# Gated linear attention and a squared-ReLU layer: the first chunks' loads interleave the batches over the partitions, and their q and k are turned by identity matmuls

## The chip, the cores and the metric

The kernel runs on one core of one Trainium2 chip. The core has a matmul engine (TensorE, PE, with a separate row PEld for its weight loads), a vector engine (DVE), a scalar engine (ACT), GpSimd (POOL) and SyncE (SP), on whose queue all the DMAs here are issued. The engines run side by side and wait for each other by semaphores. The metric is the device time of one execution in microseconds.

## The reference

Two stages. The first is a recurrence for 4 batches, 8 heads, 768 steps and head dimension 48: the state of a head (48x48) is scaled by rows with alpha, the outer product of k and v is added, and the output is q times the state. The second takes the 3072 tokens of 384 values through a layer of 2048 hidden values:

```python
for t in range(S):
    state = alpha[:, :, t, :, None] * state + np.einsum('bhd,bhe->bhde', k[:, :, t], v[:, :, t])
    y[:, :, t] = np.einsum('bhd,bhde->bhe', q[:, :, t], state)
x = y.transpose(0, 2, 1, 3).reshape(B * S, H * D)
out = np.maximum(x @ w_in, 0) ** 2 @ w_out
```

All inputs and the output are fp32 in device memory.

## The kernel before

The 768 steps of a batch are cut into 6 chunks of 128, which makes 24 chunks in all. Within a chunk the recurrence is solved by matmuls. With the running sum of ln(alpha), q is multiplied by its exponential A and k by the exponential of its negative (Ainv). The scores of all pairs of steps are then a matmul of the two products, a mask (`utri_b`) keeps the earlier steps, and the masked scores times v give the output (`py`). A state per batch carries the rest from chunk to chunk. The matmul needs the products with the head dimension on the partitions, so each product is turned by TensorE first, into PSUM, and copied to SBUF as bf16 (`qkT`).

The second stage (`add_moe1`, `add_moe2`) takes a chunk's output, turned into `xT_big`, through w_in (48 matmuls of 128 columns per chunk), relu on ACT, the square on DVE, and w_out (16 matmuls of 384 columns per chunk). Both weights are loaded as fp32 blocks (`load_w`, L297) into a pool `stage` of 5 buffers and cast to bf16 (`e_cast`, L316) by GpSimd, DVE or ACT.

The first chunk of each of the four batches (chunks 0 to 3) is treated jointly, and this is where the change lies. These four chunks need no state from before. `add_joint_load` (L357) loads alpha, q and k of all four into three tiles `atJ`, `qtJ`, `ktJ` of 128 partitions, four transfers each. A partition holds four consecutive steps of one batch (r = 0 to 3, next to each other, so each piece read is 4x48 fp32 = 768 bytes), and partition 32b+i holds batch b, steps 4i to 4i+3. Each transfer thus fills 32 neighbouring partitions:

```python
src = SRC4[nm][:, :, 0:P, :].rearrange("b h (i r) d -> b i h (r d)", r=JN)
pin(nc.sync.dma_start(out=J[nm][JP * b:JP * b + JP], in_=src[b]))
```

`add_joint` (L366) then works on all batches at once: two Ln on ACT (L371), four running sums (one for each r) by matmuls with the masks `le_b` and `lt_b`, which hold the order of steps inside each batch's block of partitions, eight exponentials on ACT (L409), eight products on DVE (L414). Each product (r and q or k) is turned by four transposes (one for each pair of heads), into one bf16 PSUM tile, and one copy (L428 on ACT, L430 on DVE) brings the tile to `qkT_j`. In `qkT_j` the columns of a batch run by step, 4i+r, so the copy for one r writes every fourth bf16 element.

`add_chunk` goes on for each chunk: the scores (`e_p2`), the masking of their two halves (`e_sm`, L588, on DVE; for chunks 1 and 3 the second half goes by an ACT copy and a GpSimd mask instead, as `SMP` says), the output, its cast `xn`, its turn and `xT_big` (L549, L551). `add_shuffle` (L439) moves k's joint products by DMA to one tile per batch, which the state of the batch needs.

The order is written out by a planner that runs while the program is built (`Plan`, L76). Every operation has an engine or a choice of engines, a duration, what it depends on, which PSUM bank it takes and a priority. The planner plays them through in time and fixes the order on each engine: on an engine, of the operations that can start first, the one with the lowest priority number. `DMA_ORDER` fixes the order of the loads on SP. In front of the first matmul, and in gaps of its plan before the second stage has begun, it puts matmuls on a zero tile (`warm`). PSUM has eight banks: two for scores (`ps_sc`), one for the state, five that are handed out (`banks`).

Of the kernel before, what the change touches and what calls it, by code (L numbers as in the profile page):

```python
# [156 lines left out]
def kernel(  # L157
# [38 lines left out]
    ps_sc = ctx.enter_context(tc.tile_pool(name="ps_sc", bufs=1, space=PSUM))  # L196
    ps_st = ctx.enter_context(tc.tile_pool(name="ps_st", bufs=1, space=PSUM))
    banks = [ctx.enter_context(tc.tile_pool(name=f"bank{i}", bufs=1, space=PSUM)) for i in range(5)]
# [18 lines left out]
    sel4 = consts.tile([P, 64], BF16)  # L217
    nc.gpsimd.tensor_copy(le_b, utri_f)
    nc.gpsimd.affine_select(
        out=lt_b, in_=le_b, compare_op=ALU.is_ge, fill=0.0,  # L220
        base=-1, pattern=[[1, P]], channel_multiplier=-1,
    )
    for b in range(JN - 1):
        blk = slice(JP * b, JP * b + JP)
        nc.vector.memset(le_b[blk, JP * b + JP:], 0.0)
        nc.vector.memset(lt_b[blk, JP * b + JP:], 0.0)
    nc.vector.memset(sel4, 0.0)  # L227
    for b in range(JN):
        nc.vector.memset(sel4[JP * b:JP * b + JP, b:b + 1], 1.0)
# [42 lines left out]
    sl_sc = Slots(1)  # L272
# [21 lines left out]
    W_CUT = {"i": [0, 2, 4, 8, 12, 16], "o": [0, 4, 8, 12, 16]}  # L294
    SB = 5

    def load_w(which):  # L297
        j = len(w_ready[which])
        lo, hi = W_CUT[which][j:j + 2]
        n = hi - lo  # L300
        box = {}

        def halves(t):
            return t.rearrange("p j (a f) -> p a j f", a=2) if which == "i" else t
        if which == "i":
            src, dst = w_in_r[:, :, lo * P:hi * P], w_in_b[:, :, lo * P:hi * P]
            shape = [P, KT, n * P]
        else:
            src, dst = w_out_r[:, lo:hi, :], w_out_b[:, lo:hi, :]
            shape = [P, n, d_model]  # L310

        def e_issue():
            box["w"] = stage.tile(shape, FP32, name=f"w{which}{n}", tag="stage")
            pin(nc.sync.dma_start(out=box["w"], in_=src))

        def e_cast():  # L316
            if op.eng == "POOL":
                pin(nc.gpsimd.tensor_copy(dst, box["w"]))
            elif op.eng == "DVE":
                pin(nc.vector.tensor_copy(halves(dst), halves(box["w"])))  # L320
            else:
                pin(nc.scalar.copy(dst, box["w"]))
        prev = w_cast[-SB] if len(w_cast) >= SB else None
        ld = add("DMA", WLD * n / 4 + 0.03, e_issue, prev, lat=2.0)
        op = add({"POOL": 0.1 + 0.46 * n, "DVE": 0.1 + 0.2 * n, "ACT": 0.1 + 0.32 * n}, 0, e_cast, ld, prio=-3.0)
        w_cast.append(op)
        w_ready[which].append(op)
# [9 lines left out]
    SC_BANKS = [sl_sc, Pair(sl_bank[2], sl_bank[3])]  # L337
    sl_sc.bank = None
    SMP = (1, 3)
    EARLY_BANKS = sl_bank[0:4]  # L340
# [16 lines left out]
    def add_joint_load(nm):  # L357
        src = SRC4[nm][:, :, 0:P, :].rearrange("b h (i r) d -> b i h (r d)", r=JN)

        def ld(b):  # L360
            if b == 0:
                J[nm] = stage.tile([P, H, JN * D], FP32, name=nm + "J", tag="stage")
            pin(nc.sync.dma_start(out=J[nm][JP * b:JP * b + JP], in_=src[b]))  # L363
        J["ld_" + nm] = [add("DMA", JLD, lambda b=b: ld(b), lat=2.0, at=0.6) for b in range(JN)]

    def add_joint():  # L366
# [7 lines left out]
        def e_tot():  # L374
            J["tot"] = psum(tot, [P, 512], FP32)
            for p in range(NP):
                for r in range(JN):
                    mm(J["tot"][:, JN * p:JN * (p + 1)], lhsT=L_j[:, r, 2 * p:2 * p + 2, :], rhs=sel4[:, 0:JN],
                       start=(r == 0), stop=(r == JN - 1), skip_group_check=True)
        tot = plan.add(Op("PE", 0.42, e_tot, lns, prio=-9.0, takes=GLA_BANKS, lat=0.05))  # L380
# [5 lines left out]
        x0 = add("ACT", 0.19, lambda: e_ae(0), tot, prio=-9.0)  # L386
        J["ae"] = tot.gives = add("ACT", 0.19, lambda: e_ae(1), tot, after(x0), prio=-9.0)

        ends = {"q": [], "k": []}

        def add_turn(r):
# [9 lines left out]
            for key, sc, prod, nm, j0 in (("q", 1.0, qA_j, "qt", 0), ("k", -1.0, kI_j, "kt", NP)):  # L401
                a, end = add_half(r, d, p0, a, key, sc, prod, nm, j0)
                ends[key].append(end)
            p0.gives = a

        def add_half(r, d, p0, a, key, sc, prod, nm, j0):
# [3 lines left out]
            a_ = add("ACT", 0.38, e_A, p0, *([after(a)] if a else []), prio=-10.0 + r * 0.001)  # L410
# [4 lines left out]
            m = add({"DVE": 0.47, "POOL": 0.95} if (key, r) in POOL_MUL else "DVE", 0.47, e_mul, a_, *J["ld_" + nm], prio=-10.0 + r * 0.001)  # L415
            J["use_" + nm] = m

            def e_tr():
                d["p" + key] = psum(tp, [P, 2 * NP, P], BF16)
                for p in range(NP):  # L420
                    tr(d["p" + key][:, p, :], prod[:, r, 2 * p:2 * p + 2, :], ident_bf)
            tp = plan.add(Op("PE", 0.22, e_tr, [m], takes=EARLY_BANKS, prio=-10.0 + r * 0.001, lat=0.15))

            def e_cp():
                o = qkT_j[:, j0:j0 + NP].rearrange("p j b (i r) -> p j b i r", r=JN)[:, :, :, :, r]
                i = d["p" + key][:, 0:NP, :].rearrange("p j (b i) -> p j b i", b=JN)
                if cp.eng == "ACT":
                    pin(nc.scalar.copy(o, i))  # L428
                else:
                    pin(nc.vector.tensor_copy(o, i))  # L430
            cp = add({"ACT": 0.49, "DVE": CPJ}, 0, e_cp, tp, prio=-10.0 + r * 0.001)
            tp.gives = cp
            return a_, cp
        for r in range(JN):
            add_turn(r)
        J["T"] = ends["q"] + ends["k"]
        w_cast.extend([lns[-1], J["use_qt"], J["use_kt"]])

    def add_shuffle(b):  # L439
        def sh():  # L440
            pin(nc.sync.dma_start(out=kn(b), in_=kI_j[JP * b:JP * b + JP]))
        J["kn", b] = [add("DMA", 0.38, sh, J["use_kt"], lat=2.0)]
# [90 lines left out]
    def add_chunk(s):  # L533
# [36 lines left out]
        def e_p2():  # L570
            x = getattr(p2.slot, "slots", None)
            if x is None:
                sc = ps_sc.tile([P, 2, NP, P], FP32, name="sc")
                sc = [sc[:, 0], sc[:, 1]]
            else:
                sc = [banks[sl.bank].tile([P, NP, P], FP32, name=f"bank{sl.bank}") for sl in x]
            d["sc"] = sc
# [5 lines left out]
        p2 = d["p2"] = plan.add(Op("PE", 0.42, e_p2, J["T"] if joint else [cp], takes=SC_BANKS if joint else [sl_sc], lat=0.10, **g))  # L583
# [76 lines left out]
    M2_LAST = sl_bank[::-1]  # L660
# [92 lines left out]
    DMA_ORDER = ["at", "qt", "kt", (0, "vt"), (1, "vt"), "i", (2, "vt"), "i", (3, "vt"), "i", "i", "i", "sh0", "sh1", "sh2", "sh3", "o", "o", 4, "o", "o", 5]  # L753
# [61 lines left out]
    for _ in range(7):  # L815
        mm(wp, lhsT=warm[:, 0:P], rhs=warm, start=True, stop=True)
    pe_end = WARM_END
# [43 lines left out]
```

## Time and profile before

| | |
|---|---|
| median of 3 runs | 196.13 us (195.58 to 196.45) |
| the profiled execution | 195.68 us, span 194.0 us |
| busy, share of the span | PE 95%, PEld 72%, DVE 67%, ACT 65%, POOL 11% |
| chain that ended last | PE 86%, DMA 6%, ACT 3%, DVE 1% |
| read from device memory, written | 25.17 MB, 4.72 MB |
| first matmul with w_in, first with w_out | 25.31 us, 37.21 us from the span's start |
| end of the last matmul | 190.1 us |

The page divides the span into 40 slices of 4.85 us and gives the busy tenths of each engine. The row PEclk is the clock that TensorE was granted, in tenths of full speed. A row of the groups names the line, the engine, the operation, the tile written and the tiles read with their shapes, the count, and after the bar the busy time in us, the mean ns of one, and the idle time before them with its cause. The chain of waits lists start, length, and what it was. Times in it are us from the start of the span. Matmul ends are modelled; an engine that is idle but not awaited costs nothing.

### The profile page before, as it was taken

Reading aid. Unit: us, or ns where it says so; the run is one execution under the profiler, and the core shown is the slowest. Engines: PE = TensorE matmul, PEld = TensorE weight load, DVE = VectorE, ACT = ScalarE, POOL = GpSimd, SP = SyncE. Lnnn points to the kernel's source line nnn. Section 1 sums busy time; section 2 is a strip of 40 time slices with the busy share of each in tenths; the row PEclk is TensorE's granted clock in tenths of the full one; section 3 lists DMA queues with packets and bytes.
Section 4 is the critical chain, followed back from the end, with each engine's and each line's share of the span. In section 5 each row is a group of like instructions: output and inputs, shape, how many; then the busy total and the mean of one; then the engine's idle time right before and its main releaser. Section 6 shows DMA issues by size and latency. Waiting matters only on the chain.

```text
span 194.0 us, 5260 instructions
## 1 busy us (share of the span) xinstructions
PE 184.6 (95%) x2103; PEld 140.4 (72%) x2103; DVE 130.6 (67%) x278; ACT 126.8 (65%) x285; POOL 21.4 (11%) x45
## 2 busy tenths in 40 slices
PE   7678899999999999999999999999999999999992
PEld 2446699866897787967867868868868768768660
DVE  2058698884899897967858758787767757735100
ACT  2389598924897588976956955954955846718210
POOL 8004520101101111111210110110110000000000
PEclk9997999999999999999999999999999999999999
DMA  6999999799999998999989899751110110111111
GB/s 127 208 201 277 351 377 272 169 329 176 208 249 208 179 217 168 230 177 219 204 175 222 175 211 235 143 129 39 41 45 0 46 42 3 41 41 44 40 57 66
DMA packets 98793, 30.75 MB, mean 159 GB/s; under 512 B 88144, under 2 KB 97616, under 8 KB 98768
## 3 DMA queue, kind: packets, MB, share of 16 engines
q1 hardware_dynamic: 98768, 30.42, 67.6%
q8 instruction: 16, 0.26, 0.6%
q14 instruction: 9, 0.07, 0.1%
HBM read 25.17 MB, written 4.72 MB: 154 GB/s over the span
## 4 chain that ended last, share of the span: by engine, by line
PE 86%; DMA 6%; ACT 3%; DVE 1%; SPq 1%; issue 0%; DVEq 0%
PE bank L266 74%; PE bank L269 7%; DMA ktJ<-in_k_dram 4%; PE sc L266 4%; ACT gT L428 3%; DMA atJ<-in_alpha_dram 2%; PE st L266 2%; DVE sm L588 1%; SPq L363 1%; DVE gT L414 0%; ACT xT_big L549 0%; ACT ob L744 0%; ACT ae_j L385 0%; DVEq L414 0%
## 5 line engine op out<-in xcount | busy, mean ns | idle before, releaser
L266 PE MATMUL bank<-xT_big,w_in_b 128*128 128x256 bf16 (+1 forms) x720 | 76.5, 251 | 0.0
L266 PE MATMUL bank<-w_out_b,gT 128*128 128x384 bf16 x384 | 71.8, 326 | 0.0
L692 ACT ACTIVATE r<-bank 128x512 bf16<-128x512 f32 x96 | 56.7, 604 | 16.4 <-PE bank L266 14.4
L266 PEld LDWEIGHTS <-w_in_b 128*128 128x128 bf16 x720 | 55.2, 98 | 4.9
L266 PEld LDWEIGHTS <-gT 128*128 128x128 bf16 (+1 forms) x432 | 36.4, 97 | 19.9 <-ACT gT L428 0.8
L702 DVE TENSOR_TENSOR gT<-r 128x512 bf16<-128x512 bf16 x96 | 39.8, 433 | 15.8 <-ACT r L692 15.5
L588 DVE TENSOR_TENSOR sm<-sc,utri_b 128x512 bf16<-128x512 f32 x44 | 28.2, 682 | 3.4 <-PE sc L266 3.3
L563 POOL CAST vb<-vt 128x384 bf16<-128x384 f32 x21 | 11.8, 563 | 117.3 <-DMA vt<-in_v_dram 66.2
L744 ACT COPY ob<-bank 128x384 f32<-128x384 f32 x21 | 10.1, 483 | 19.7 <-PE bank L266 19.6
L508 DVE TENSOR_TENSOR qA_s<-qt,A 128x384 bf16<-128x384 f32 x20 | 11.1, 557 | 9.6 <-ACT A L489 9.5
L551 DVE COPY qkT<-bank 128x1024 bf16<-128x1024 bf16 x20 | 13.8, 689 | 5.5 <-PE bank L269 5.4
L463 ACT CAST sb<-st 128x384 bf16<-128x384 f32 x20 | 9.5, 476 | 8.2 <-DVE st L458 8.2
L549 ACT CAST xn<-bank 128x384 bf16<-128x384 f32 x24 | 11.6, 481 | 4.5 <-PE bank L266 4.4
L266 PEld LDWEIGHTS <-qkT 64*128 64x128 bf16 (+1 forms) x240 | 10.0, 95 | 5.6 <-issue 2.4
L266 PE MATMUL bank<-warm 128*128 128x256 bf16 (+1 forms) x59 | 12.7, 361 | 1.3 <-DVE sel L227 1.3
L489 ACT ACTIVATE A<-bank 128x384 bf16<-128x384 f32 x20 | 10.0, 500 | 4.3 <-PE bank L266 4.2
L556 ACT ACTIVATE L_s<-at 128x384 bf16<-128x384 f32 x20 | 10.4, 522 | 1.9 <-DMA at<-in_alpha_dram 1.6
L511 DVE TENSOR_TENSOR kI_s<-kt,Ainv 128x384 bf16<-128x384 f32 x20 | 11.0, 551 | 0.0
L266 PEld LDWEIGHTS <-warm 128*128 128x128 bf16 x59 | 6.7, 121 | 4.7 <-issue 2.2
L493 ACT ACTIVATE Ainv<-bank 128x384 bf16<-128x384 f32 x20 | 10.1, 504 | 0.0
L266 PEld LDWEIGHTS <-sm 128*128 128x128 bf16 x192 | 8.5, 96 | 1.8 <-issue 0.3
L551 DVE COPY xT_big<-bank 128x384 bf16<-128x384 bf16 x21 | 7.3, 350 | 3.6 <-PE bank L269 3.6
(74 smaller groups left out, 173.7 us busy)
## 6 DMA issues: line engine op xcount, KB each, us to landing
vt<-in_v_dram SPq DMA_DIRECT2D x24, 192.0 KB, 4.0
out_dram<-ob SPq DMA_DIRECT2D x24, 192.0 KB, 3.0
at<-in_alpha_dram SPq DMA_DIRECT2D x20, 192.0 KB, 4.0
qt<-in_q_dram SPq DMA_DIRECT2D x20, 192.0 KB, 4.0
kt<-in_k_dram SPq DMA_DIRECT2D x20, 192.0 KB, 3.7
wo<-in_moe_w_out_dram SPq DMA_DIRECT2D x4, 768.0 KB, 7.8
wi<-in_moe_w_in_dram SPq DMA_DIRECT2D x3, 768.0 KB, 7.9
atJ<-in_alpha_dram SPq DMA_DIRECT2D x4, 192.0 KB, 3.9
```

The source lines that it names most:

```text
L266: pin(nc.tensor.matmul(*a, **kw))
L269: pin(nc.tensor.transpose(*a))
L493: pin(nc.scalar.activation(d["Ai"], d["pm"][:, 0:HD].rearrange("p (h d) -> p h d", h=H), AF.Exp, scale=-1.0))
L508: pin(nc.vector.tensor_mul(qA[:, :, 0:D], d["qt"], d["A"]))
L511: pin(nc.vector.tensor_mul(kI[:, :, 0:D], d["kt"], d["Ai"]))
L549: pin(nc.scalar.copy(out_t, in_t))
L551: pin(nc.vector.tensor_copy(out_t, in_t))
L556: pin(nc.scalar.activation(L[:, :, 0:D], d["at"], AF.Ln))
L563: pin(nc.gpsimd.tensor_copy(d["vb"], d["vt"]))
L588: pin(nc.vector.tensor_mul(d["sm"][:, hh], d["sc"][hh], utri_b.to_broadcast([P, NP, P])))
L692: pin(nc.scalar.activation(box["r"][:, 0:w], box["ph"][:, 0:w], AF.Relu))
L702: pin(nc.vector.tensor_mul(gT[g][:, f0:f0 + per, lo * P:lo * P + n], r, r))
```

## The change

The joint tiles interleave the batches: partition 4i+b holds batch b, steps 4i to 4i+3, so a transfer fills every fourth partition. The masks `le_b` and `lt_b` follow: a matmul of a small tile `own` with itself gives 1 where two partitions are of the same batch, and DVE multiplies this with the triangle. `sel4` is now the last four columns of `le_b`.

The turn works by pair of heads instead of by r: for q or k and one pair, four identity matmuls (one for each r) write into one fp32 PSUM tile, each to every fourth column, so that the columns stand in the order of steps; one copy then brings 128x512 fp32 to contiguous bf16. Each such group needs all four products of q or of k. The priorities put q's products ahead of k's, and the totals of the chunks (`tot`) behind all of them.

The scores lose their own pool: `banks` has seven entries, scores use banks 5 and 6 as a pair, and the running sums and turns at the start may use them too. All masks are made on DVE (`SMP` is empty). The third block of w_in is cut into two, and the planner may not put the first three casts of w_in on ACT, nor the first two on DVE (the list `w_cast` already holds three entries then), so the first two go to GpSimd.

```diff
@@ -193,9 +193,8 @@

-    ps_sc = ctx.enter_context(tc.tile_pool(name="ps_sc", bufs=1, space=PSUM))
     ps_st = ctx.enter_context(tc.tile_pool(name="ps_st", bufs=1, space=PSUM))
-    banks = [ctx.enter_context(tc.tile_pool(name=f"bank{i}", bufs=1, space=PSUM)) for i in range(5)]
+    banks = [ctx.enter_context(tc.tile_pool(name=f"bank{i}", bufs=1, space=PSUM)) for i in range(7)]

@@ -214,19 +213,13 @@
     lt_b = consts.tile([P, P], BF16)
-    sel4 = consts.tile([P, 64], BF16)
-    nc.gpsimd.tensor_copy(le_b, utri_f)
+    own = consts.tile([JN, JP, JN], BF16)
+    nc.gpsimd.memset(own, 0.0)
     nc.gpsimd.affine_select(
-        out=lt_b, in_=le_b, compare_op=ALU.is_ge, fill=0.0,
-        base=-1, pattern=[[1, P]], channel_multiplier=-1,
+        out=own, in_=own, compare_op=ALU.not_equal, fill=1.0,
+        base=0, pattern=[[0, JP], [1, JN]], channel_multiplier=-1,
     )
-    for b in range(JN - 1):
-        blk = slice(JP * b, JP * b + JP)
-        nc.vector.memset(le_b[blk, JP * b + JP:], 0.0)
-        nc.vector.memset(lt_b[blk, JP * b + JP:], 0.0)
-    nc.vector.memset(sel4, 0.0)
-    for b in range(JN):
-        nc.vector.memset(sel4[JP * b:JP * b + JP, b:b + 1], 1.0)
+    sel4 = le_b[:, P - JN:P]
     ones_t = consts.tile([P, 32], BF16)
@@ -269,7 +262,6 @@
     plan = Plan()
-    sl_sc = Slots(1)
     sl_bank = [Slots(1) for _ in banks]
@@ -291,8 +283,10 @@
     w_cast = []
-    W_CUT = {"i": [0, 2, 4, 8, 12, 16], "o": [0, 4, 8, 12, 16]}
+    W_CUT = {"i": [0, 2, 4, 6, 8, 12, 16], "o": [0, 4, 8, 12, 16]}
     SB = 5
+    NO_ACT = 6
+    NO_DVE = 5

@@ -322,7 +316,12 @@
         ld = add("DMA", WLD * n / 4 + 0.03, e_issue, prev, lat=2.0)
-        op = add({"POOL": 0.1 + 0.46 * n, "DVE": 0.1 + 0.2 * n, "ACT": 0.1 + 0.32 * n}, 0, e_cast, ld, prio=-3.0)
+        on = {"POOL": 0.1 + 0.46 * n, "DVE": 0.1 + 0.2 * n, "ACT": 0.1 + 0.32 * n}
+        if len(w_cast) < NO_DVE:
+            del on["DVE"]
+        if len(w_cast) < NO_ACT:
+            del on["ACT"]
+        op = add(on, 0, e_cast, ld, prio=-3.0)
         w_cast.append(op)
@@ -334,10 +333,10 @@
     POOL_MUL = ()
-    SC_BANKS = [sl_sc, Pair(sl_bank[2], sl_bank[3])]
-    sl_sc.bank = None
-    SMP = (1, 3)
-    EARLY_BANKS = sl_bank[0:4]
+    EARLY_BANKS = sl_bank[0:4] + sl_bank[5:7]
+    SC = Pair(sl_bank[5], sl_bank[6])
+    SC_BANKS = [SC, Pair(sl_bank[2], sl_bank[3])]
+    SMP = ()
     EARLY = 4
@@ -360,7 +359,7 @@
                 J[nm] = stage.tile([P, H, JN * D], FP32, name=nm + "J", tag="stage")
-            pin(nc.sync.dma_start(out=J[nm][JP * b:JP * b + JP], in_=src[b]))
+            pin(nc.sync.dma_start(out=J[nm][b::JN], in_=src[b]))
         J["ld_" + nm] = [add("DMA", JLD, lambda b=b: ld(b), lat=2.0, at=0.6) for b in range(JN)]
@@ -375,18 +374,15 @@
                 for r in range(JN):
-                    mm(J["tot"][:, JN * p:JN * (p + 1)], lhsT=L_j[:, r, 2 * p:2 * p + 2, :], rhs=sel4[:, 0:JN],
+                    mm(J["tot"][:, JN * p:JN * (p + 1)], lhsT=L_j[:, r, 2 * p:2 * p + 2, :], rhs=sel4,
                        start=(r == 0), stop=(r == JN - 1), skip_group_check=True)
-        tot = plan.add(Op("PE", 0.42, e_tot, lns, prio=-9.0, takes=GLA_BANKS, lat=0.05))
+        tot = Op("PE", 0.42, e_tot, lns, prio=-9.0, takes=GLA_BANKS, lat=0.05)

...
             pin(nc.scalar.activation(ae_j[rows, :, :, j], t, AF.Exp))
-        x0 = add("ACT", 0.19, lambda: e_ae(0), tot, prio=-9.0)
-        J["ae"] = tot.gives = add("ACT", 0.19, lambda: e_ae(1), tot, after(x0), prio=-9.0)
-
-        ends = {"q": [], "k": []}
+        muls = {"q": [], "k": []}

@@ -398,47 +394,58 @@
             a = None
-            for key, sc, prod, nm, j0 in (("q", 1.0, qA_j, "qt", 0), ("k", -1.0, kI_j, "kt", NP)):
-                a, end = add_half(r, d, p0, a, key, sc, prod, nm, j0)
-                ends[key].append(end)
+            for key, sc, prod, nm in (("q", 1.0, qA_j, "qt"), ("k", -1.0, kI_j, "kt")):
+                a = add_half(r, d, p0, a, key, sc, prod, nm)
             p0.gives = a

-        def add_half(r, d, p0, a, key, sc, prod, nm, j0):
+        def add_half(r, d, p0, a, key, sc, prod, nm):
+            g = dict(prio=-10.0 + r * 0.001 + (0.01 if key == "k" else 0.0))
+
             def e_A():
...
                 pin(nc.scalar.activation(d["A" + key], d["pm"][:, 0:HD].rearrange("p (h d) -> p h d", h=H), AF.Exp, scale=sc))
-            a_ = add("ACT", 0.38, e_A, p0, *([after(a)] if a else []), prio=-10.0 + r * 0.001)
+            a_ = add("ACT", 0.38, e_A, p0, *([after(a)] if a else []), **g)

...
                 pin(e.tensor_mul(prod[:, r, :, 0:D], J[nm][:, :, r * D:(r + 1) * D], d["A" + key]))
-            m = add({"DVE": 0.47, "POOL": 0.95} if (key, r) in POOL_MUL else "DVE", 0.47, e_mul, a_, *J["ld_" + nm], prio=-10.0 + r * 0.001)
+            m = add({"DVE": 0.47, "POOL": 0.95} if (key, r) in POOL_MUL else "DVE", 0.47, e_mul, a_, *J["ld_" + nm], **g)
             J["use_" + nm] = m
+            muls[key].append(m)
+            return a_
+
+        def add_turned(key, p, prod, j0):
+            g = dict(prio=(-9.97 if key == "q" else -9.96) + p * 0.001)
+            d = {}

             def e_tr():
-                d["p" + key] = psum(tp, [P, 2 * NP, P], BF16)
-                for p in range(NP):
-                    tr(d["p" + key][:, p, :], prod[:, r, 2 * p:2 * p + 2, :], ident_bf)
-            tp = plan.add(Op("PE", 0.22, e_tr, [m], takes=EARLY_BANKS, prio=-10.0 + r * 0.001, lat=0.15))
+                d["pT"] = psum(tp, [P, JN * P], FP32)
+                for r in range(JN):
+                    o = d["pT"].rearrange("p (b i r) -> p r i b", b=JN, r=JN)[:, r]
+                    mm(o, lhsT=prod[:, r, 2 * p:2 * p + 2, :], rhs=ident_bf, start=(r == 0), stop=True, skip_group_check=True)
+            tp = plan.add(Op("PE", 0.22, e_tr, muls[key], takes=EARLY_BANKS, lat=0.15, **g))

             def e_cp():
-                o = qkT_j[:, j0:j0 + NP].rearrange("p j b (i r) -> p j b i r", r=JN)[:, :, :, :, r]
-                i = d["p" + key][:, 0:NP, :].rearrange("p j (b i) -> p j b i", b=JN)
+                o = qkT_j[:, j0 + p]
+                i = d["pT"].rearrange("p (b t) -> p b t", b=JN)
                 if cp.eng == "ACT":
...
                     pin(nc.vector.tensor_copy(o, i))
-            cp = add({"ACT": 0.49, "DVE": CPJ}, 0, e_cp, tp, prio=-10.0 + r * 0.001)
-            tp.gives = cp
-            return a_, cp
+            cp = tp.gives = add({"ACT": 0.49, "DVE": CPJ}, 0, e_cp, tp, **g)
+            return cp
         for r in range(JN):
             add_turn(r)
-        J["T"] = ends["q"] + ends["k"]
+        plan.add(tot)
+        x0 = add("ACT", 0.19, lambda: e_ae(0), tot, prio=-9.0)
+        J["ae"] = tot.gives = add("ACT", 0.19, lambda: e_ae(1), tot, after(x0), prio=-9.0)
+        tot.deps += [(m, None) for m in muls["q"] + muls["k"]]
+        J["T"] = [add_turned("q", p, qA_j, 0) for p in range(NP)] + [add_turned("k", p, kI_j, NP) for p in range(NP)]
         w_cast.extend([lns[-1], J["use_qt"], J["use_kt"]])
...
         def sh():
-            pin(nc.sync.dma_start(out=kn(b), in_=kI_j[JP * b:JP * b + JP]))
+            pin(nc.sync.dma_start(out=kn(b), in_=kI_j[b::JN]))
         J["kn", b] = [add("DMA", 0.38, sh, J["use_kt"], lat=2.0)]
@@ -568,19 +575,13 @@
         def e_p2():
-            x = getattr(p2.slot, "slots", None)
-            if x is None:
-                sc = ps_sc.tile([P, 2, NP, P], FP32, name="sc")
-                sc = [sc[:, 0], sc[:, 1]]
-            else:
-                sc = [banks[sl.bank].tile([P, NP, P], FP32, name=f"bank{sl.bank}") for sl in x]
-            d["sc"] = sc
+            sc = d["sc"] = [banks[sl.bank].tile([P, NP, P], FP32, name=f"bank{sl.bank}") for sl in p2.slot.slots]
             t = qkT_j[:, :, b] if joint else d["qkT"]
...
                     mm(sc[hh][:, p, :], lhsT=t[sl, NP + p], rhs=t[sl, p], start=True, stop=True)
-        p2 = d["p2"] = plan.add(Op("PE", 0.42, e_p2, J["T"] if joint else [cp], takes=SC_BANKS if joint else [sl_sc], lat=0.10, **g))
+        p2 = d["p2"] = plan.add(Op("PE", 0.42, e_p2, J["T"] if joint else [cp], takes=SC_BANKS if joint else [SC], lat=0.10, **g))

@@ -657,7 +658,7 @@
     FIRST = sl_bank[4:0:-1]
-    M2_LAST = sl_bank[::-1]
+    M2_LAST = sl_bank[4::-1]
     OUT_LATE = 3.5
@@ -750,7 +751,7 @@

-    DMA_ORDER = ["at", "qt", "kt", (0, "vt"), (1, "vt"), "i", (2, "vt"), "i", (3, "vt"), "i", "i", "i", "sh0", "sh1", "sh2", "sh3", "o", "o", 4, "o", "o", 5]
+    DMA_ORDER = ["at", "qt", "kt", (0, "vt"), (1, "vt"), "i", (2, "vt"), "i", (3, "vt"), "i", "i", "i", "i", "sh0", "sh1", "sh2", "sh3", "o", "o", 4, "o", "o", 5]
     for d in DMA_ORDER + list(range(6, NT)):
@@ -812,8 +813,16 @@
     wp = banks[4].tile([P, 512], FP32, name="bank4")
-    for _ in range(7):
+    for i in range(7):
         mm(wp, lhsT=warm[:, 0:P], rhs=warm, start=True, stop=True)
+        if i == 3:
+            same = banks[0].tile([P, P], FP32, name="bank0")
+            mm(same, lhsT=own, rhs=own, start=True, stop=True)
+    nc.vector.tensor_mul(le_b, same, utri_b[:, 0, :])
+    nc.gpsimd.affine_select(
+        out=lt_b, in_=le_b, compare_op=ALU.is_ge, fill=0.0,
+        base=-1, pattern=[[1, P]], channel_multiplier=-1,
+    )
     pe_end = WARM_END
...
```

## The prediction

> **What bounds the kernel now.** I read the slices of the page first, then the chain of waits in order of time, then the rows of the first 31 us, the windows, and the transfers' landing times. From the page:
>
> ```profile
> PE   7678899999999999999999999999999999999992
> PEclk9997999999999999999999999999999999999999
> DMA  6999999799999998999989899751110110111111
> GB/s 127 208 201 277 351 377 272 169 329 176 208 249 208 179 217 168 230 177 219 204 175 222 175 211 235 143 129 39 41 45 0 46 42 3 41 41 44 40 57 66
> ```
>
> TensorE is full from the sixth slice on. After 26.6 us the answer on waits shows no idle of the matmul row, and the last matmul ends at 190.1. So the end moves with the moment at which dense work starts, unless something makes holes behind it. That moment is the first w_in matmul, at 25.31. The chain before it:
>
> ```profile
> 2.22 4.74 DMA atJ<-in_alpha_dram
> 6.98 7.77 DMA ktJ<-in_k_dram
> ...
> 15.92 3.59 ACT gT L428 x3
> ...
> 19.73 1.31 ACT gT L428
> 21.04 0.05 issue
> 21.09 0.42 PE sc L266 x8
> 21.53 1.30 DVE sm L588 x2
> ```
>
> The joint loads own the chain until 14.78, the scattered copies of the turned products until 21.04, then masks, output, transpose until 25.31. The rows (engine, operation, count; busy us, mean ns):
>
> ```profile
> L428 ACT COPY gT<-bank 128x512 bf16<-128x512 bf16 x6 | 7.5, 1338 | 0.2
> L430 DVE COPY gT<-bank 128x512 bf16<-128x512 bf16 x2 | 2.6, 1302 | 0.3 <-PE bank L269 0.3
> L593 ACT CAST sm<-bank 128x512 bf16<-128x512 f32 x2 | 1.2, 586 | 1.2 <-PE bank L266 1.2
> L551 DVE COPY qkT<-bank 128x1024 bf16<-128x1024 bf16 x20 | 13.8, 689 | 5.5 <-PE bank L269 5.4
> L318 POOL CAST w_in_b<-wi 128x768 bf16<-128x768 f32 x1 | 1.0, 1012 | 0.7 <-DMA wi<-in_moe_w_in_dram 0.7
> ```
>
> A copy of 512 elements that scatters costs 1.3 us; a contiguous one of 512 on ACT 0.59, and of 1024 on DVE 0.69.
>
> **Loads.** The last alpha transfer lands at 2.22+4.74 = 6.96, the last k transfer at 14.78, eight transfers later: 0.98 us per 196.6 KB, 201 GB/s. The rate is not the queue's limit: w_in's second and third 768 KB blocks land 2.05 us apart (384 GB/s, 2 KB rows), and the four loads of the sixth chunk (192-byte rows) 0.87 us apart. Per packet of one of 16 engines that is 85 ns for 2 KB and 13.6 ns for 192 B; on the line between them 768 B take 36 ns, and 16 of them 0.57 us. That is my estimate if the 32 neighbouring partitions are what holds these loads; the other end is no change, 0.98 us (a loss I exclude: bytes, row length and packets stay, and the kernel's full-partition loads run at these rates). I take 0.57, because 201 GB/s is below even the short-packet rows and the destination is the one thing that sets these transfers apart from them. The first transfer lands at 3.8 as now. Then alpha ends at 3.8+3x0.57 = 5.5, q at 7.8, k at 3.8+11x0.57 = 10.1: 4.7 us earlier. SP issues one in 0.44 to 0.49 us, so it still keeps ahead.
>
> [...]
>
> **Products.** Ln took 7.07 to 8.65; now 5.6 to 7.2. From Ln's end to the first exponential it is 0.89 us, then eight at a pitch of 0.375: last start 10.7, last end 11.2. The fourth turn no longer waits for a bank (now it starts its first exponential at 12.59): there are six early banks instead of four. Products on DVE at 0.55 each: from 10.1, six remain (one of q's third, the last q and four of k), so q's end at 11.8 and k's at 13.4, against 17.92.
>
> **Turn.** Eight groups of four transposes become eight groups of four identity matmuls of the same 128 columns; a group now takes 0.40 from first to last end and some 0.22 of pitch. New is the fp32 output at a stride of four. No row has a strided PSUM output. Lower bound: no dearer, 0.22 a group. Upper bound: by the scattered copies against the straight one on ACT 1338/586 = 2.3, on DVE 1302 against half of 689 = 3.8 times, so 0.85. I take twice, 0.45, by the ACT row, which is the nearest in that only the order of the output differs. q's groups run 11.8 to 13.6 while k's products are made, k's 13.6 to 15.4. The copies fall to 0.59 on ACT and at most 0.68 on DVE (masks of 512 fp32, two inputs). q's are hidden behind k's groups on the otherwise empty ACT; the last k copy adds 0.7: the scores start at 16.1, not 21.09. At 0.22 it would be 15.1, at 0.85 19.3 (11.8+6.8+0.7).
>
> [...]
>
> **From scores to dense work.** Now 25.31-21.09 = 4.22. Without the ACT copy of chunk 1's scores (0.59, in front of the first x evacuation) some 0.3 goes: first w_in matmul at 16.1+3.9 = 20.0, 5.3 earlier. Against that, all eight masks are on DVE (two of 0.68 added, two copies of 0.59 on ACT and two masks of 1.15 on GpSimd removed). They follow each other, 5.3 us in place of 4; the fourth chunk's x comes later by up to 1. TensorE has other chunks' columns to work on meanwhile: I charge 0.5. Net 4.8.
>
> **Edits costed at nothing.** Masks le/lt: `own` replaces a GpSimd cast of 0.29, one small matmul goes in among the warming ones, one DVE product and one GpSimd select of 0.29 follow behind the memsets that end at 5.3 now; ready near 5.7, needed at Ln's end, 7.2. If GpSimd were 1.5 us later, each further us would cost one. Behind `own`'s wait on TensorE stand three warming matmuls only. The chunk totals go behind the products; their exponentials serve the state at 30.34, and end at 19.7 now. w_in blocks 1 and 2 on GpSimd: 1.01 each; landing 17.5 and 19.6 now, 4.7 earlier then, so done by 16 with two v casts of 0.5 behind them, against 20.0. DVE gives up its 0.58. Cutting the third block in two adds an issue on SP (about 0.5) and a cast; the sixth block waits for the first one's cast, and behind it on SP stand the shuffles and w_out, but the queues then hold megabytes. Reading the shuffles' source at stride four moves the same bytes. The score pair in banks 5 and 6 and the last outputs' five banks are the old ones renamed.
>
> **What is late next.** The transfers. w_out's third block is cast at 41.33 and its first matmul, the 33rd of that stage, runs at 43.9; 1.6 us of slack behind the cast. The whole queue moves up 4.7, less 0.2 for two loads with 1 KB rows; a shift of TensorE over 4.5+1.6 = 6.1 would turn into a wait. 4.8 is inside.
>
> Sum on the profiled execution: 195.68-4.8 = 190.9. The median of the runs stands 0.45 above that execution; half of it, as the profile lies inside the runs' own spread, gives 191.1.
>
> **Rivals.**
> 1. The loads don't speed up (their 768-byte pieces of HBM, or something per transfer, hold them at 0.98). For: the source is read as before, and the DMA share is already 1.1 to 1.2 there. Against: the rows above. Then k lands at 14.78, q's turn is hidden, four k products end at 17.1, k's groups overlap them not at all: 17.1+1.8+0.7 = 19.6 for the scores, 1.5 earlier; with 0.3 and -0.5 a gain of 1.3, 194.6.
> 2. All goes better: contiguous price (6.3 at the first w_in matmul), no loss on masks, capped at 6.1 by w_out, and a little from faster loads (0.50 each, 393 GB/s, about the best row): down to 188.3.
> 3. Slower: the strided outputs dominate. With x us a group the scores start at 11.8+8x+0.7; less 0.3 and plus 0.5, that passes 21.09 at x = 1.05, 0.26 us per matmul against 0.055 now, nearly five times. At eight times (1.76) they start at 26.6, 5.7 later: 202. Against: both scattered rows stay under four times.
> 4. TensorE's clock: it falls to 0.50 between 17 and 20 us now. If that falls on the first w_in matmuls, 3 us at half speed cost 1.5: 192.6.
>
> **How the numbers follow.** Forecast with its own range (188.9 to 193) 0.60; rival 1 0.13; rival 2 0.12; rival 4 0.08; rival 3 and its half-way forms 0.07, of which 0.02 land at no change. Within 0.5% (1 us) is what a measurement can't tell from nothing. Rival 1 reaches it in a quarter of its cases, so faster 0.90, same 0.05, slower 0.05. The range goes from rival 2 to rival 1's end: 188.3 to 194.6, with about 0.13 outside.
>
> **What would show it.** Right: last k transfer landing near 10, 0.6 between landings, copies of the products at 0.6, first scores at 15 to 17, first w_in matmul at 19 to 21, no TensorE idle after. Wrong: landings still 0.98 apart; identity matmuls that follow each other by over 0.2 us; TensorE waiting on w_in or w_out casts; a clock of 0.5 past 20 us.

## The result and the profile after

The changed kernel took 193.12 us (median of 4 runs, 192.80 to 193.99) against 196.28 for the kernel before on the same chip; the ratio is 0.985, 95% interval 0.981 to 0.989. The forecast was 191.1: faster, as said, but 3 us gained instead of 5. The profiled execution took 193.14 us with a span of 191.4, so 2.5 us less than the profiled one before.

The slices of the page after (busy tenths in 40 slices of 4.8 us, the granted clock, the share of the DMA engines, the rate):

```profile
PE   7989999999999998999999999999999999999992
PEclk9999999999999999999999999999999999999999
DMA  4999999997999997989999999440110110111111
GB/s 123 270 279 308 362 372 205 311 194 155 263 212 200 215 220 142 236 167 240 180 221 232 185 235 211 83 134 0 44 42 0 46 41 5 41 45 41 41 59 66
```

The second and third slices moved 208 and 201 GB/s before and move 270 and 279 now; the clock's dip in the fourth slice is gone. New is an 8 in TensorE's row at the sixteenth slice, 72 to 77 us, far behind everything that was changed. The chain of waits, its beginning:

```profile
7.51 0.61 SPq L362
8.12 0.04 issue
8.17 4.01 DMA ktJ<-in_k_dram
...
12.30 1.04 DVE gT L411 x2
13.34 0.05 issue
13.38 5.32 PE bank L259 x64
18.70 1.29 DVE sm L589 x2
```

The long stretch of scattered copies on ACT has left the chain, as forecast. In its place stands SP's queue: twelve issues of 0.61 us in a row, and only then the last k transfer. Last k landing, first scores, first w_in matmul, start of the last evacuation: 14.78, 21.09, 25.31, 190.14 before; 12.18, 18.26, 21.79, 187.66 after. Dense work thus begins 3.5 us earlier, and the end comes 2.5 us earlier: one microsecond is lost on the way.

The groups of the turn after (from 12 to 19 us; count, then busy us and mean ns of one):

```profile
L259 PE MATMUL bank<-ident_bf,gT 128*128 128x128 bf16 x32 | 4.0, 310 | 0.9 <-DVE gT L411 0.9
...
L432 ACT CAST gT<-bank 128x512 bf16<-128x512 f32 x5 | 2.8, 587 | 2.9 <-PE bank L259 2.9
L434 DVE CAST gT<-bank 128x512 bf16<-128x512 f32 x3 | 2.1, 688 | 0.7 <-PE bank L259 0.7
```

The copies cost 0.59 on ACT and 0.69 on DVE instead of 1.34 and 1.30.

### The profile page after: what moved, and what is told of

It is laid out like the page before. It is cut to its first block, busy times and chain, and to the rows that moved or that the text cites. A ratio compares the mean times of both kernels' runs of the same rounds, so it can differ in the third digit from the quotient of the medians.

```text
span 191.4 us, 5250 instructions
## 1 busy us (share of the span) xinstructions
PE 184.5 (96%) x2104; PEld 140.9 (74%) x2104; DVE 128.1 (67%) x268; ACT 123.1 (64%) x284; POOL 21.3 (11%) x46
## 4 chain that ended last, share of the span: by engine, by line
PE 83%; SPq 5%; DMA 5%; DVE 3%; issue 1%; ACT 1%; DVEq 0%
PE bank L259 75%; PE bank L262 6%; SPq L362 4%; DMA at<-in_alpha_dram 3%; DMA ktJ<-in_k_dram 2%; PE st L259 2%; DVE sm L589 1%; SPq L480 1%; DVE gT L411 1%; DVE qA_s L515 0%; ACT r L693 0%; DVE kI_s L518 0%; ACT ob L745 0%; DVE gT L703 0%; SPq L750 0%
## 5 line engine op out<-in xcount | busy, mean ns | idle before, releaser
L259 PEld LDWEIGHTS <-gT 128*128 128x128 bf16 (+1 forms) x464 | 39.8, 100 | 20.5 <-DVE gT L411 1.2
L589 DVE TENSOR_TENSOR sm<-bank,utri_b 128x512 bf16<-128x512 f32 x48 | 30.5, 682 | 2.4 <-PE bank L259 2.4
L745 ACT COPY ob<-bank 128x384 f32<-128x384 f32 x21 | 10.1, 483 | 19.3 <-PE bank L259 19.3
L515 DVE TENSOR_TENSOR qA_s<-qt,A 128x384 bf16<-128x384 f32 x20 | 11.2, 559 | 10.1 <-ACT A L496 10.1
L259 PE MATMUL bank<-warm 128*128 128x256 bf16 (+1 forms) x59 | 11.0, 334 | 1.3 <-DVE warm L202 1.3
L500 ACT ACTIVATE Ainv<-bank 128x384 bf16<-128x384 f32 x20 | 10.1, 503 | 0.0
L259 PEld LDWEIGHTS <-warm 128*128 128x128 bf16 x59 | 6.0, 110 | 4.2 <-issue 1.6
```

Source lines behind the costliest of these rows:

```text
L259: pin(nc.tensor.matmul(*a, **kw))
L500: pin(nc.scalar.activation(d["Ai"], d["pm"][:, 0:HD].rearrange("p (h d) -> p h d", h=H), AF.Exp, scale=-1.0))
L515: pin(nc.vector.tensor_mul(qA[:, :, 0:D], d["qt"], d["A"]))
L589: pin(nc.vector.tensor_mul(d["sm"][:, hh], d["sc"][hh], utri_b.to_broadcast([P, NP, P])))
```

## The experiments

Two theories for the lost microsecond run through them. S: the end is held by the stream of transfers, which TensorE runs into far behind the changed part. T: the new masks and the new plan lose it. A third question is what holds the joint loads. All comparisons are ratios to the kernel before on the same chip, with 95% intervals.

**Loads alone.** The kernel before, with the new placement, the masks and the shuffle's source, but the old turn:

```diff
-            pin(nc.sync.dma_start(out=J[nm][JP * b:JP * b + JP], in_=src[b]))
+            pin(nc.sync.dma_start(out=J[nm][b::JN], in_=src[b]))
...
-                i = d["p" + key][:, 0:NP, :].rearrange("p j (b i) -> p j b i", b=JN)
+                i = d["p" + key][:, 0:NP, :].rearrange("p j (i b) -> p j b i", b=JN)
```

> The kernel before, with only the interleaved joint loads (and the masks and the shuffle that follow from them); its transposes, scattered copies, casts and GpSimd masks stay. Theory S (the end moves with the stream of transfers, which TensorE catches up with near 74 us): the last k transfer lands at 12.2, first w_in matmul near 22.7, and the time is that of the full change, 193.1 +- 0.4, though dense work starts 0.9 later than there. Theory T (the end moves with the start of dense work, and the 0.8 us lost later belong to masks and plan): first w_in matmul 22.7, so 0.9 slower than the full change, 194.0 or more.

Ratio 0.993 (0.991 to 0.995), 194.22 us. The last k issue is at 8.2 and lands 4.1 later as in the full change, but the scattered copies still fill ACT, scores start at 19.53 and w_in at 23.75, a microsecond later than I expected. From there to the last evacuation (188.59) it takes 164.84 us, and the kernel before took 164.83. So with a lead of 1.56 us at the start, all of it arrives at the end. The full change has a lead of 3.52 and takes 165.87. (These lengths are each of one profiled execution.) The time itself spoke for T, the missing loss for S; it didn't decide.

**Turn alone.** The changed kernel with the joint loads on neighbouring partitions again:

```diff
-            pin(nc.sync.dma_start(out=J[nm][b::JN], in_=src[b]))
+            pin(nc.sync.dma_start(out=J[nm][JP * b:JP * b + JP], in_=src[b]))
```

> The changed kernel with the joint loads put back on 32 neighbouring partitions each (masks, totals and shuffle with them); turn, priorities, casts and masks on DVE stay. The last k transfer lands at 14.8 again, scores near 19.6 in place of 21.09, first w_in matmul near 23.3, 2 us earlier than before. Theory S: the stream is not earlier, so most of it is given back: 195.5 to 196.3. Theory T: 194.3 to 194.8.

Ratio 0.999 (0.996 to 1.003). I missed the reason: w_in starts at 25.44, not at 23.3, so there is no lead to lose. DVE's order has k's first product ahead of q's last, since the planner takes 0.59 us for a joint load and thinks k is there. With k landing at 14.31, q's last product and with it q's whole turn wait for k. TensorE stands idle for 2.35 us, and the clock that it is granted next is about half:

```profile
15.49 2.96 PE L265 MATMUL bank<-ident_bf,gT 128*128 128x128 bf16 x13 [2.35 <-DVE gT L417]
```

```profile
13.00:15.00 2.00, 0.15 (x2) 0.00 (x0) 0.59 (x2) 0.00 (x0) 0.00 (x0) 1.00 1.40 208
15.00:17.00 2.00, 1.50 (x8) 1.51 (x9) 2.00 (x4) 0.80 (x2) 1.17 (x2) 0.56 1.11 269
```

The first line is from the timeline; the other two are windows (start, end, us, busy us of PE, PEld, DVE, ACT, POOL, the clock, the DMA share, GB/s). In the window after the idle time the clock is 0.56, and 13 matmuls take 2.96 us that take 1.59 in the full change. That the idle time is what lowers the clock is not shown: with q on ACT's queue, the run that follows, TensorE idles for longer and the clock stays at 1.00. The turn alone is worth nothing here; together with the loads it brings 2 us at the first w_in matmul (21.79 against 23.75).

**q on ACT's queue.** The changed kernel, one line:

```diff
-            pin(nc.sync.dma_start(out=J[nm][b::JN], in_=src[b]))
+            pin((nc.scalar if nm == "qt" else nc.sync).dma_start(out=J[nm][b::JN], in_=src[b]))
```

> The changed kernel with the four joint q transfers issued on ACT's queue instead of SP's, so that the issues of 0.61 us no longer stand in one line. If the issue sets the pace of the joint loads: the last k transfer lands at 10.1 to 10.6 instead of 12.18, and by theory S the whole stream and the end come 1.5 to 2 us earlier, 191.2 to 191.7. If the transfers themselves take 0.66 to 0.76 us each: k lands at 11.8 or later and the time stays at 193.1.

Ratio 1.001 (0.997 to 1.004): all of the gain gone. The transfers do run faster, 312 to 352 GB/s from 6 to 10 us against 245 to 304 in the full change. But q's transfers now run beside alpha's, and alpha, which everything waits for, lands last at 9.0 instead of 6.1; Ln starts at 9.07, w_in at 24.25. K lands at 11.7, half a microsecond earlier. These landings are those of the profiled execution, the fastest of ten (194.42 against a median of 196.11); its last evacuation is still 0.8 us earlier than before the change, and what the other nine lose more is not shown. In it TensorE waits 3.81 us for the Ln, and the clock reads 1.00 in every window up to 16 us:

```profile
10.70 0.32 PE L259 MATMUL bank<-gT,le_b 128*128 128x384 bf16 x1 [3.81 <-ACT gT L370]
```

**Batches alternating between the queues.** To free the issue and keep the order:

```diff
+            pin((nc.scalar if b % 2 else nc.sync).dma_start(out=J[nm][b::JN], in_=src[b]))
```

> The changed kernel with the joint transfers of batches 1 and 3 issued on ACT's queue and those of 0 and 2 on SP's, so that alpha, q and k keep their order on both. If one queue's issue (0.656 us each with its gap) holds the joint loads: alpha lands near 5.3, k at 10.2 to 10.8, first w_in matmul at 20.0 to 20.6, and the end 1.3 to 2 us earlier than the change, 191.2 to 191.9. If the transfers hold themselves: k at 11.7 or later, first w_in matmul at 21.4 or later, 192.7 or more.

Ratio 0.980 (0.971 to 0.988), which can't be told from the change's 0.985. Alpha lands at 7.4, as one transfer of ACT's queue takes 5.9 us; k at 12.9; w_in starts at 22.54. The issue of k was not freed, though:

```profile
L362 ACTq DMA_DIRECT2D ktJ<-in_k_dram x2: 607/616/626, 7.6 to 8.2; - x2
```

ACT issued its two k transfers only after it had waited for alpha and begun the first Ln (7.54). So the late k of this run says nothing about what a free issue would bring.

**One transfer for each joint tile.**

```diff
+            pin(nc.sync.dma_start(out=J[nm], in_=src))
```

> The changed kernel with each joint tile loaded by one transfer of 768 KB to all 128 partitions in place of four; the planner's length for it is four times that of one. If the issue costs per instruction: three issues of about 0.7 us, k lands at 10 to 10.5 and the time is 191 to 192. If it costs per piece that it describes: each takes 2.4 us, k lands near 12.2 as now, and the time is 193 +- 0.5.

Ratio 0.984 (0.978 to 0.989). The issues of the first two took 0.73 and 0.65 us for four times the bytes, which spoke for a price per instruction; the third, k's, took 2.37, the figure of the other case:

```profile
L362 SPq DMA_DIRECT2D ktJ<-in_k_dram x1: 2373/2373/2373, 2.3 to 2.3; - x1
```

So neither case holds for all three; why the third took longer is not shown. It was over at 4.7 us all the same, where the change's last issue starts at 8.17, and k lands at 11.8. The slice from 4.8 to 9.6 us moves 334 GB/s, which is 0.59 us per 196.6 KB, my estimate. So with the issue earlier the transfers reach the rate that I took (each is four times as large here, too), and yet k lands only 0.4 us earlier, in all three variants between 11.7 and 12.9. In this one alpha too comes later (6.9); q follows at 9.3 and k at 11.8, 0.60 and 0.62 us per 196.6 KB. By the windows of 1 us some 2.7 MB had moved when k landed, 0.34 more than the three tiles hold, and v's first loads were issued from 4.7 on, so a part of the time may be theirs. Why the last landing trails the bytes by so much is open.

**Neighbouring columns.** The changed kernel with the turn's order made by the copy's read instead of the matmul's write:

```diff
-                    o = d["pT"].rearrange("p (b i r) -> p r i b", b=JN, r=JN)[:, r]
+                    o = d["pT"][:, r * P:(r + 1) * P]
...
-                o = qkT_j[:, j0 + p]
-                i = d["pT"].rearrange("p (b t) -> p b t", b=JN)
+                o = qkT_j[:, j0 + p].rearrange("p b (i r) -> p b i r", r=JN)
+                i = d["pT"].rearrange("p (r i b) -> p b i r", b=JN, r=JN)
```

> The changed kernel with the identity matmuls writing 128 neighbouring fp32 columns each; the copy reads every fourth one instead. If the strided output is what makes these matmuls follow each other at 0.10 us, they now do at 0.06 or less and the last group ends 0.6 us earlier; if the weight loads (0.097 each) set it, the pitch stays at 0.10. Copies: 0.6 to 0.7 if reading PSUM at a stride is free, over 1 if not. Theory S: time within 0.3 us of 193.1 whichever way. Theory T: it follows the scores' start, 192.5 or 194 and more.

Ratio 0.987 (0.982 to 0.993), within 0.3 us of the change's median (193.35). The row of the identity matmuls in this run:

```profile
L259 PE MATMUL bank<-ident_bf,gT 128*128 128x128 bf16 x32 | 2.6, 220 | 1.6 <-DVE gT L411 1.6
```

220 ns each instead of 310, and thirteen in 0.90 us instead of 1.59. So the strided output does cost: each of the twelve pitches takes (0.90-0.22)/12 = 0.057 us against (1.59-0.31)/12 = 0.107, close to twice. Why it costs, no run shows. Nor do the weight loads set the pitch, which is now below the 0.097 us of each in this run (PEld's `<-gT`, 12 to 19 us). The copies that read at the stride cost the same as before, 592 and 683 ns. The scores start 0.24 us earlier (0.92 in the run with a shorter lead below, which has the same turn; here k's products took 854 ns in the median, there 705), w_in at 21.55, and the last evacuation at 187.51: the lead over the kernel before grows to 3.76, what arrives stays near 2.6. That spoke for S.

**Long rows.** The changed kernel, with the loads of chunks 4 to 23 reading neighbouring bytes (the chunk gets other values; the number of bytes is the same):

```diff
+                flat = RAW[nm].rearrange("b h s d -> b (h s d)")[b, c * n:(c + 1) * n]
+                pin(nc.sync.dma_start(out=d[nm].rearrange("p h d -> p (h d)"), in_=flat.rearrange("(p f) -> p f", p=P)))
```

> The changed kernel with the loads of the chunks from 4 on taken as 128 rows of 1536 neighbouring bytes each, in place of 1024 pieces of 192; the bytes and the buffers stay, but the chunk gets other steps and heads than the reference's, so its values are not computed. Theory S (TensorE runs into the stream of short packets near 74 us): the wait on alpha there goes, and 0.5 to 0.9 us comes back, 192.2 to 192.6. Theory T (masks and plan take it): 193.1 +- 0.3.

Ratio 0.978 (0.972 to 0.984), 192.63 us. The interval overlaps that of the change (0.981 to 0.989), so the time alone does not show it. W_in starts at 22.09, later than in the full change, as k lands 0.3 us later, and the last evacuation at 187.14, earlier: 165.05 us, 0.2 above the kernel before. What has gone is seen in the timeline of ACT. Three lines, each the ninth Ln of the chunks from 4 on: before, the full change, and the long rows.

```profile
76.27 0.52 ACT L556 ACTIVATE L_s<-at 128x384 bf16<-128x384 f32 x1 [0.57 <-DMA at<-in_alpha_dram]
```

```profile
73.85 0.52 ACT L563 ACTIVATE L_s<-at 128x384 bf16<-128x384 f32 x1 [1.37 <-DMA at<-in_alpha_dram]
```

```profile
72.70 0.53 ACT L569 ACTIVATE L_s<-at 128x384 bf16<-128x384 f32 x1
```

In the full change ACT stands 1.37 us before this Ln until the chunk's alpha has landed. Behind it in ACT's order is a relu, and behind that on DVE a square and the masks that TensorE waits for. The chain of the full change passes here too:

```profile
68.48 5.35 DMA at<-in_alpha_dram
73.83 0.02 issue
73.85 0.02 ACT L_s L563
```

This Ln stands 2.42 us earlier than before, and the end 2.48. TensorE's own order shows how much goes here. Two of its operations, one before the wait and one behind it, before and in the full change:

```profile
75.44 0.33 PE L266 MATMUL st<-vb,kI_s 128*128 128x96 bf16 x4
79.11 0.32 PE L266 MATMUL bank<-L_s,utri_b 128*128 128x384 bf16 x1
```

```profile
72.25 0.33 PE L259 MATMUL st<-vb,kI_s 128*128 128x96 bf16 x4
76.69 0.32 PE L259 MATMUL bank<-L_s,utri_b 128*128 128x384 bf16 x1
```

The first is still 3.19 us ahead of the kernel before, the second 2.42: 0.77 of the lost 1.04 us go at this place. With the long rows the Ln has no wait. This is S, shown at its place. Whether the engines' rate or SP's issues hold the short rows there isn't separated, as the long rows shorten both (SP's issues between 62 and 67 us take 0.3 to 0.5, those in front of this alpha in the full change 0.4 to 1.1). The remaining 0.3 is open; the runs with the new plan in which no such Ln waits for alpha (this one, the turn alone, and q on ACT's queue; one execution of each) take 165.05 to 165.27, those with the old plan 164.83 to 164.97, so some of it may be the plan's. The same rows on the kernel before:

> The kernel before with the loads of the chunks from 4 on as 128 rows of 1536 bytes (their values are not computed, as in the run of the same change on the new kernel). Theory S says that the old kernel's dense work starts just late enough not to run into the stream: the waits on alpha near 74 to 76 us go, and the time stays within 0.5 us of the kernel before. If the stream of short rows already held the old kernel, it gains 0.7 us or more.

Ratio 0.999 (0.997 to 1.002), 164.97 us from w_in to the last evacuation. The short rows cost the old kernel nothing that these runs resolve: its dense work starts just late enough.

**Masks split again.** `SMP = (1, 3)` in the changed kernel.

> The changed kernel with the masks of chunks 1 and 3 split again between DVE and ACT with GpSimd. If all masks on DVE cost the 0.3 to 0.5 us that the plan loses between the first w_in matmul and the steady part, that comes back in the steady part, and the time is 192.7 or less; by theory S the end stays at 193.1 +- 0.4 whichever way.

Ratio 0.984 (0.979 to 0.990). Nothing came back: w_in starts at 22.67, from scores at 18.46 that is 4.2 us as in the kernel before, against 3.53 with all masks on DVE. The dense stage takes 165.91 us, no less than in the full change. T falls for the masks.

**A shorter lead.** `LEAD = 3.0` instead of 3.5, with the neighbouring columns.

> The changed kernel with the identity matmuls to neighbouring columns and the planner's lead of the recurrence over the second stage cut from 3.5 chunks to 3.0, so that TensorE asks for each chunk's loads some 2 to 3.5 us later and has second-stage work in the meantime. Theory S: the wait on alpha near 74 us shrinks, the end comes 0.4 to 1 us earlier than the changed kernel, ratio 0.980 to 0.983. If the loads are not what is late there: ratio 0.985 or, for want of a lead, more.

Ratio 0.986 (0.983 to 0.990): a miss. W_in starts at 20.87, 4.4 us earlier than before, and the last evacuation at 187.97, 2.2 earlier. Ln waits for alpha at 45.86, 63.96, 68.63, 73.68 and 77.71, more often than in the full change. Asking in another order didn't relieve the waits.

**q's last product first.** `JLD = 0.76` in the planner, with the neighbouring columns.

> The changed kernel with the identity matmuls to neighbouring columns (as in the run of that alone) and the planner told 0.76 us per joint load instead of 0.59, which puts q's last product ahead of k's first. q's turn no longer waits for k's landing at 12.2, so scores should start 0.3 to 0.8 us earlier than with the first of the two alone (18.0), first w_in matmul near 21.0. Theory S: the end is set by the alpha transfer of the chunk near 74 us and stays within 0.4 us of the changed kernel's ratio, 0.985. If dense work's start sets it: ratio 0.982 or less.

Ratio 0.990 (0.986 to 0.994). Scores start at 16.53 and w_in at 20.06, 5.25 us earlier than before, and the end comes 1.8 us earlier, less than in the full change. The place of the loss is another one, so S as I had put it, with the alpha near 74, is too narrow. TensorE's waits from 18 us on:

```profile
PE st L259 <- DMA kI_s<-gT: 0.8, 1, 0.8
PE bank L259 <- DVE qkT L558: 0.5, 1, 0.5
PE bank L259 <- ACT w_in_b L316: 0.5, 1, 0.5
```

It now waits already for the shuffle of k's products, which lands at 27.1 after 8.6 us in the queues. With the long rows on top:

> The kernel with neighbouring columns and 0.76 in the planner, whose dense work starts at 20.06 (5.25 us earlier than before) and which ends only 1.8 us earlier, now with the loads of the chunks from 4 on as 128 rows of 1536 bytes (their values are not computed). Theory S: with the stream of short rows gone, the end follows the start of dense work again, as in the runs that have no wait on alpha (165.0 us from first w_in matmul to last evacuation): most of 5.25 comes back, ratio 0.975 or less. If the plan itself loses it: ratio 0.985 or more.

Ratio 0.984 (0.980 to 0.989): a miss, with neither case met. The profiled execution is the slowest of the five (194.32 us against a median of 192.74), so its lengths need not be those of the others. It waits 2.17 us for the same shuffle (18.88+9.69 = 28.57), and its dense stage takes 168.65 us from the first w_in matmul. The long rows did not shorten this wait (0.8 us without them); that it accounts for the miss is not shown. The plan puts the state's matmul in TensorE's order where it expected the shuffle; whether another order would find work there wasn't tried.

## Why the prediction was right or wrong

**Loads: right in direction, the size failed.** The step was "SP issues one in 0.44 to 0.49 us, so it still keeps ahead". The issues before and after, from the answers on the alpha tile (ns, minimum, median, maximum):

```profile
L363 SPq DMA_DIRECT2D atJ<-in_alpha_dram x4: 389/441/450, 0.8 to 2.2; - x4
```

```profile
L362 SPq DMA_DIRECT2D atJ<-in_alpha_dram x4: 607/614/738, 0.8 to 2.9; - x4
```

The same bytes to every fourth partition take 0.61 us to issue, 0.656 with the gap, more than the 0.57 that the transfer was to take. The last issue starts at 8.17; with the 3.0 us to landing of the first transfer k would be there at 11.2, so 1.1 us of the delay are the issues'. Landing takes 4.0 us there, and this other microsecond is not explained. So k lands at 12.18, not at 10.1: 2.1 us, the largest part of the error. I moved the destination and left the issue at its old price. That the issue was all that held k is not so: with one transfer per tile the issues were over at 4.7, and k landed at 11.8. The cause that I gave for the slow loads, their placement, stands by the two runs that split the change: with the loads alone k lands near 12.3 (8.2+4.1), with the turn alone at 14.31. The slices that moved 208 and 201 GB/s before move 270 and 279 in the full change, and one moves 334 with one transfer per tile; why the placement matters, no run shows. My estimate of 0.57 us per transfer is close to the spacing then seen, 0.60 and 0.62; that alpha was there only at 6.9 in that run, not at 5.5, no term of the sum held.

**Products and turn: the prices right, the path right by luck.** Scores were to start 6.0 us after k's landing; they start 6.08 after it. But the 6.0 counted two of q's products as still to be made when k lands at 10.1. With k at 12.18 they could have been done, and q's turn hidden before k, as rival 1 has it: 2.3+1.8+0.7 = 4.8 us, scores at 17.0. What happened instead stands in DVE's order after the change:

```profile
12.30 0.56 DVE L411 TENSOR_TENSOR gT<-ktJ,Ainv 128x384 bf16<-128x384 f32 x1 [0.90 <-DMA ktJ<-in_k_dram]
12.77 0.55 DVE L411 TENSOR_TENSOR gT<-qtJ,A 128x384 bf16<-128x384 f32 x1
```

q's last product stands behind k's first and waits for its landing, and q's turn with it, as in the run of the turn alone. The run that mends this order starts its scores at 16.53, against 18.02 and 17.34 in the two others with neighbouring columns: 0.8 to 1.5 us that belong to the order. The sum had no term for it, and came out because its own wait for q had about that size (6.0-4.8 = 1.2). The doubled price of the strided output was taken from an ACT row of another kind and met the measured pitch (0.11 assumed, 0.107 found). Copies of 0.59 and 0.68 were met.

**From scores to dense work: better than said.** 3.53 us, not 3.9: without the split of the masks 0.7 goes, not 0.3, by the run that puts it back (4.2). The 0.5 charged for the masks on DVE wasn't paid there: the first w_out matmul is at 33.78 against 37.21, so 3.43 of the lead of 3.52 still stands.

**What is late next: right kind, wrong place.** I put the limit of the transfers at w_out's third block and at 6.1 us of lead. It binds at the alpha of a chunk near 74 us, and about 2.5 of the lead is left behind it. I had worked out that limit from one load with its slack, where the stream of the 192-byte rows that follows runs on at full share until 120 us; the kernel before already waited there, 0.57 us at 76.27, and its page shows the row, `L_s<-at` with 1.6 us of waits for alpha, which the sum gave no term.

**The sum.** 5.3 at the first w_in matmul less 2.1 for k's landing plus 0.3 gives the measured 3.5; less 1.0 behind it, instead of 0.5, gives 2.5 in the profiled executions. Of the signs named, the copies at 0.6 came; k near 10, scores at 15 to 17 and w_in at 19 to 21 did not. The measured 193.12 lies just past the 188.9 to 193 that had 0.60, and inside the wide range only by the end that rival 1 gave it, though that rival didn't occur. Nor did the others: the loads did speed up, the strided outputs were twice and not five times as dear, and the clock stayed up. Open are the late landing in the change itself and with one transfer, and what besides the shuffle (TensorE's recorded waits add up to 2.0 us) lengthens the dense stage of the last two variants to over 168 us.

## What to carry to other kernels

When a change moves where a transfer lands, price its issue anew as well as its bytes, and the time from issue to landing beside them: here the issues made about half of the delay, and the rest lay between issue and landing. A lead won at the start is worth only what the loads behind it can follow, so look in the profile for places where an engine that TensorE depends on already waits for a transfer, however short the wait, and expect the lead to shrink there: here 0.57 us of waiting grew to 1.37. An order written out by a planner fits only the durations it was given: one product stood behind a load that came late, which left the turn alone without a gain and cost the whole change some of its own. When one term of a sum comes out right although its path was another, look which two errors cancelled.

## What the runs showed of the hardware

- A transfer of 196.6 KB to every fourth partition took 0.61 us to issue (the median of each joint tile in the full change), to 32 neighbouring ones 0.44, 0.45 and 0.38 (alpha, q and k before). Three of 786 KB to all 128 in a row took 0.73, 0.65 and 2.37.
- Alpha's last landing went from 6.1 to 9.0 us when q was issued on ACT's queue beside it.
- Identity matmuls that write every fourth fp32 column of PSUM followed each other at 0.107 us in the full change, with neighbouring columns at 0.057 in the run of those. There the copies of ACT and DVE read the same stride from PSUM in 592 and 683 ns, against 587 and 688 for neighbouring columns.
- After 2.35 us without a matmul the granted clock was 0.56 in the next window of the run of the turn alone; after 3.81 us without one it was 1.00 in the profiled run with q on ACT's queue. So in these two runs the length of the gap alone doesn't tell.
